# A planned order for attention and gated MLP on one core: loads tied to the first score, the last output unit in three parts

## The chip, the cores and the metric

The kernel runs on one core of a Trainium2 chip. The metric is the device time of one execution in microseconds (us). A core has five engines: PE (TensorE, with its weight loads shown apart as PEld), DVE (VectorE), ACT (ScalarE), POOL (GpSimd) and SP (SyncE), each with a queue of its own that runs in program order, and 16 DMA engines which all queues share. Matmul results land in PSUM and are copied to SBUF by DVE or ACT.

## The reference

Four batches, eight heads, 768 tokens, head dimension 64. An 8x8 matrix per head is normalized by rows and columns five times and then mixes the eight blocks of 96 tokens of k and v. Attention runs inside each block. Its output, 768x512 per batch, goes through a gated MLP whose gate mixes tokens.

```python
for _ in range(5):                       # P: (B, H, 8, 8)
    P = exp(P - max(P, -1)); P /= sum(P, -1) + 1e-9; P /= sum(P, -2) + 1e-9
k_s = einsum('bhij,bhjcd->bhicd', P, k_blocks)     # v_s in the same way
attn = softmax(q_b @ k_s.T / sqrt(64)) @ v_s       # within each block
x = attn as (4, 768, 512)
h = relu(x @ w_in)                       # 512 -> 1024
u, v = h[..., :512], h[..., 512:]
v_n = (v - mean(v)) / sqrt(var(v) + 1e-6)
v_s = einsum('ts,bsd->btd', w_spatial, v_n) + b_spatial
out = (u * v_s) @ w_out                  # 512 -> 512, float32
```

## The kernel before

The instruction order of PE, DVE, ACT and POOL is written out by hand in the string `SCHEDULE`. It is a list of units. A token such as `a20-3` reads: unit `a`, number 2, batch 0, engine that evicts the result (A for ACT, D for DVE, - for a fixed one), PSUM tile 3. There are four PSUM tiles (`ps0` to `ps3`, each two banks of 512 float32 columns), so a unit waits until the unit that last had its tile is evicted. The units and their matmuls (each with its weight load):

| token | method | matmuls | what follows |
|---|---|---|---|
| k, t | `mixed_t` (L302) | 12 | mixes and transposes k or v, evicted to `kT` |
| q | `qtr` (L290) | 24 | transposes q, evicted to `qT` |
| s | `score` (L345) | 8, 96 wide | exponential on ACT to `ex` (L352) |
| z | `sums` (L364) | 4, 384 wide | logarithm and exponential on ACT to `lns` (L370, L371) |
| a | `attend` (L382) | 32, 96 wide | two products on DVE to `xt` (L392) |
| B | `vblk` (L329) | 8 | evicted to `vb` |
| v | `vmix` (L260) | 2 | evicted to `vm`, written to DRAM and read back as `vb` by SP |
| X, V | `vstart`, `vproj` (L415) | 4 for X; 8 for V, or 4 behind its X | 512 wide; `relu` on ACT, statistics on DVE |
| N | `norm` | none | two steps on ACT, six on DVE (L448) |
| U | `uproj` (L458) | 8, 384 wide | `relu` on ACT or DVE |
| S | `spatial` (L474) | 12, 384 wide | bias on DVE (L485), product on POOL (L486) to `gt` |
| O | `oproj` (L496) | 8, 512 wide | evicted to `o_sb`, stored by SP |
| w | `wsp_unit` (L226) | 6 | transposes `w_spatial` |

Batches overlap: the attention of batch b+1 is interleaved with the MLP of batch b. A stage below means such a pair. `O` uses the `gt` of all four `S` units of its batch in the order in which they are numbered.

Loads of q, k and v are issued by POOL (`load_heads`, L94), with two buffers per tensor. Those of batches 0 and 1 and of the weights are issued at the start. Those of batch b+2 are issued behind the first `S` of batch b, so behind its product on POOL's queue:

```python
if name == "S" and b + 2 < B and len(gmlp[b].gt) == 1:
    v_in[b + 2] = load_heads(v, b + 2, "v_in")
    ...
```

In the last batch each `O` unit is evicted in four copies of 128x256, alternating DVE and ACT, and stored in two DMAs of 256 KB on SP's queue. All four copies of a unit read one PSUM tile and write one SBUF tile. `lns` has four buffers.

## Time and profile before

| | |
|---|---|
| runs, us | 159.97, 163.50, 163.62 (median 163.5) |
| profiled execution, us | 165.63; its span, first to last instruction, 163.8 |
| busy in the span, us | PE 147.0, PEld 85.6, DVE 93.3, ACT 95.8, POOL 47.9 |
| granted TensorE clock, mean | 0.962 |
| instructions | 4347, of them 1888 matmuls and 1897 weight loads in the trace |
| DMA | 23.88 MB moved; read 27.14 MB, written 8.65 MB of HBM |
| q, k, v of a batch | 768 KB each in SBUF; median 13.9, 10.6, 9.6 us from issue to landing |

Views of the profile used below: the slices (the span in 40 equal parts, a digit is a busy share in tenths, PEclk the clock that was granted to TensorE), the chain of waits (the work that ended last, followed back to what released each step; "issue" is time in which an engine waited for nothing that the profile shows), the windows (per stretch: busy time of PE, PEld, DVE, ACT, POOL, with the number of instructions in brackets, then the granted clock, the mean share of the DMA engines, and GB/s), and the groups of instructions by line with the mean time of one. In a DMA row the numbers are packets, MB and the share of 16 engines' time; q0 holds POOL's loads, q1 SP's transfers, q8 instructions. Matmuls are pipelined, so the price of one in a row of equal ones is read from the chain (16 of 512 columns in 3.45 us) and not from its own mean (406 ns).

### The profile page before, as it was taken

How to read it: one execution, taken by the hardware profiler on the slowest of the kernel's cores; microseconds unless marked ns; L12 is line 12 of the kernel's file. 1: busy time of each engine (PE TensorE's matmuls, PEld its weight loads, DVE VectorE, ACT ScalarE, POOL GpSimd, SP SyncE). 2: the span in 40 equal slices, each digit the busy share in tenths (PEclk: the TensorE clock that was granted, in tenths of full speed). 3: DMA queues.
4: the chain of work that ended last, by engine and by line, in shares of the span. 5: the costliest groups of instructions: out<-in, count | busy, mean ns of one | idle time of the engine just before them, and what ended most of it. 6: DMA issues, size and time to landing. Idle time of an engine off the chain costs nothing.

```text
span 163.8 us, 4347 instructions
## 1 busy us (share of the span) xinstructions
PE 147.0 (90%) x1888; PEld 85.6 (52%) x1897; DVE 93.3 (57%) x196; ACT 95.8 (59%) x147; POOL 47.9 (29%) x45
## 2 busy tenths in 40 slices
PE   0949887999999958999999999999999999999970
PEld 0237764366765543445855554458655454566430
DVE  4777895068954382039654385396543853844751
ACT  3167992088966670567986725679867346570040
POOL 7966920000006950000009750000045600005600
PEclk9999995599999996999999999999999999999997
DMA  2999999999590999651742999817500036000055
GB/s 13 197 204 211 221 260 192 202 204 208 162 238 20 134 204 203 194 233 59 211 118 14 174 203 223 352 39 223 132 0 0 4 134 256 0 0 0 6 192 193
DMA packets 21299, 23.88 MB, mean 146 GB/s; under 512 B 736, under 2 KB 18144, under 8 KB 21152
## 3 DMA queue, kind: packets, MB, share of 16 engines
q0 software_dynamic: 13504, 12.58, 47.9%
q1 hardware_dynamic: 7776, 11.02, 20.0%
q8 instruction: 15, 0.25, 0.6%
q14 instruction: 4, 0.03, 0.1%
HBM read 27.14 MB, written 8.65 MB: 219 GB/s over the span
## 4 chain that ended last, share of the span: by engine, by line
PE 77%; DVE 8%; ACT 5%; issue 4%; POOL 3%; DMA 1%; DVEq 0%; POOLq 0%
PE ps L474 19%; PE ps L415 14%; PE ps L458 13%; PE ps L496 12%; PE ps L345 4%; PE ps L302 3%; POOL gt L486 3%; ACT ex L352 3%; PE ps L290 3%; PE ps L260 2%; PE ps L382 2%; PE ps L364 2%; DVE vs L485 2%; PE ps L226 1%; PE ps L329 1%
## 5 line engine op out<-in xcount | busy, mean ns | idle before, releaser
L486 POOL TENSOR_TENSOR gt<-vs,u_sb 128x768 bf16<-128x768 f32 x15 | 24.6, 1647 | 99.4 <-ACT ex L352 73.9
L474 PE MATMUL ps<-wspT,v_sb 128*128 128x384 bf16 x192 | 33.5, 327 | 0.0
L485 DVE TENSOR_TENSOR vs<-ps,b_bc 128x768 f32<-128x768 f32 (+1 forms) x17 | 15.5, 910 | 24.5 <-PE ps L474 24.5
L437 DVE BATCH_NORM_STATS2 stats<-v_sb 128x6 f32<-128x512 bf16 x24 | 16.2, 675 | 22.9 <-ACT v_sb L241 22.8
L352 ACT ACTIVATE ex<-ps 96x768 bf16<-96x768 f32 x32 | 24.1, 804 | 7.7 <-PE ps L345 7.7
L474 PEld LDWEIGHTS <-v_sb 128*128 128x128 bf16 x192 | 17.8, 98 | 12.3 <-issue 1.0
L496 PE MATMUL ps<-w_out_sb,gt 128*128 128x512 bf16 x90 | 23.6, 403 | 0.6
L415 PE MATMUL ps<-w_in_sb,xt 128*128 128x512 bf16 x94 | 23.8, 406 | 0.2 <-issue 0.2
L458 PE MATMUL ps<-xt,w_in_sb 128*128 128x384 bf16 x128 | 23.0, 326 | 0.1
L235 ACT COPY o_sb<-ps 128x1024 f32<-128x1024 f32 (+1 forms) x13 | 9.3, 717 | 22.0 <-DVE o_sb L237 11.8
L241 ACT ACTIVATE v_sb<-ps 128x1024 bf16<-128x1024 f32 (+1 forms) x15 | 12.4, 852 | 11.7 <-PE ps L415 11.0
L392 DVE TENSOR_TENSOR xt<-ps,lns 128x384 bf16<-128x384 f32 x32 | 15.8, 549 | 3.6 <-PE ps L382 3.3
L458 PEld LDWEIGHTS <-w_in_sb 128*128 128x128 bf16 x128 | 12.1, 98 | 8.4
L415 PEld LDWEIGHTS <-xt 128*128 128x128 bf16 x96 | 9.9, 104 | 12.5 <-issue 3.0
L496 PEld LDWEIGHTS <-gt 128*128 128x128 bf16 x96 | 9.1, 102 | 12.8 <-issue 2.3
L370 ACT ACTIVATE lns<-ps 128x384 f32<-128x384 f32 x16 | 7.8, 488 | 11.0 <-PE ps L364 11.0
L382 PE MATMUL ps<-ex,vb 96*32 96x96 bf16 x512 | 8.7, 215 | 4.0 <-issue 3.7
L241 ACT ACTIVATE u_sb<-ps 128x768 bf16<-128x768 f32 x14 | 11.2, 813 | 1.8 <-PE ps L458 1.8
L235 ACT CAST kT<-ps 128x768 bf16<-128x768 f32 x14 | 10.6, 811 | 0.9 <-PE ps L302 0.9
L382 PEld LDWEIGHTS <-vb 96*32 96x32 bf16 x512 | 7.4, 101 | 5.1 <-issue 4.0
L345 PE MATMUL ps<-qT,kT 64*96 64x96 bf16 x256 | 9.6, 210 | 0.1
L345 PEld LDWEIGHTS <-kT 64*96 64x96 bf16 x256 | 7.2, 121 | 4.3 <-issue 3.5
(73 smaller groups left out, 157.8 us busy)
## 6 DMA issues: line engine op xcount, KB each, us to landing
out_dram<-o_sb SPq DMA_DIRECT2D x9, 512.0 KB, 2.7
q_in<-in_q_dram POOLq DMA_DIRECT2D x4, 768.0 KB, 13.9
k_in<-in_k_dram POOLq DMA_DIRECT2D x4, 768.0 KB, 10.6
v_in<-in_v_dram POOLq DMA_DIRECT2D x4, 768.0 KB, 9.6
vd<-vm SPq DMA_DIRECT2D x6, 384.0 KB, 2.5
vb<-vd SPq DMA_DIRECT2D x6, 384.0 KB, 4.3
out_dram<-o_sb SPq DMA_DIRECT2D x6, 256.0 KB, 2.1
wsp_nat<-in_moe_w_spatial_dram POOLq DMA_DIRECT2D x1, 1152.0 KB, 21.4
```

Of the source, the lines that this page charges most:

```text
L235: nc.scalar.copy(out=out, in_=in_)
L241: nc.scalar.activation(out=out, in_=in_, func=AF.Relu)
L345: nc.tensor.matmul(t[0:BLK, hh, ii * BLK:(ii + 1) * BLK], lhsT=self.k[hp][rows, i * BLK:(i + 1) * BLK], rhs=self.q[hp][rows, i], start=Tru ...
L352: nc.scalar.activation(out=e.rearrange("p h i c -> p h (i c)"), in_=t[0:BLK, :, 0:NB // 2 * BLK], func=AF.Exp, scale=scale,)
L382: nc.tensor.matmul(t[c * DQ:(c + 1) * DQ, dh, ii * BLK:(ii + 1) * BLK], lhsT=self.vb[:, i, j, c, :].rearrange("c (d x) -> c x d", x=2)[:, ...
L415: nc.tensor.matmul(self.vt[n][:, x, :], lhsT=self.xt(kc)[:, g * 128:(g + 1) * 128], rhs=w_in_sb[:, kc, DH:DFF], start=(kc == 0), stop=(kc ...
L437: nc.vector.bn_stats(out=stats, in_=v_sb[:, x, :])
L458: nc.tensor.matmul(t[:, x, 0:HW], lhsT=w_in_sb[:, kc, mc * 128:(mc + 1) * 128], rhs=self.xt(kc)[:, x * HW:(x + 1) * HW], start=(kc == 0), ...
L474: nc.tensor.matmul(t[:, x, 0:HW], lhsT=self.v[g][:, mc * 128:(mc + 1) * 128], rhs=wspT[:, g, x * HW:(x + 1) * HW], start=(g == 0), stop=(g ...
L485: nc.vector.tensor_add(out=vs[:, x], in0=t[:, x, 0:HW], in1=b2[:, x])
L486: eng.tensor_mul(out=gt2[:, x], in0=vs[:, x], in1=u2[:, x])
L496: nc.tensor.matmul(t[:, x, :], lhsT=self.gt[mc][:, g * 128:(g + 1) * 128], rhs=w_out_sb[:, mc, :], start=(mc == 0), stop=(mc == FC - 1),)
```

## The change

Three things change in the code, and the order of the units changes throughout.

- The loads of batch b+1 are issued behind the first `score` of batch b, for b of 1 and 2, and POOL first copies one element of that score's `ex` tile, which makes POOL's queue wait for ACT's exponential.
- The last `O` unit of the last batch is computed in three parts (512, 256 and 256 columns wide), each in a PSUM tile and an SBUF tile of its own, with one copy and one DMA for each: the first two by ACT and SP's queue, the third by DVE and ACT's queue. The other `O` units of the last batch are evicted in one copy and stored in one DMA of 512 KB.
- `lns` has three buffers in place of four.
- `SCHEDULE` has a new order. Among other things `X10` stands ahead of `a20` in batch 0, and `O10` and `O00` stand ahead of `a31` and `a21` of batch 1. Engines and PSUM tiles of the units are newly assigned; four more `relu`s are on DVE.

```diff
-    ln_pool = ctx.enter_context(tc.tile_pool(name="ln", bufs=4))
+    ln_pool = ctx.enter_context(tc.tile_pool(name="ln", bufs=3))
...
         def oproj(self, n, eng, ps):
+            self.ops.append(ps)
             t = ps_tile(ps)
...
             if self.last and n == G // 2 - 1:
-                pairs = [(mc, x) for x in range(2) for mc in range(FC)]
...
+                free = min(set(range(4)) - set(self.ops))
+                parts = ((0, 0, DM, t), (1, 0, DM // 2, ps_tile(free)), (1, DM // 2, DM // 2, None))
+                for x, c, width, tp in parts:
+                    tp = ps_tile(self.ops[0]) if tp is None else tp
+                    g = 2 * n + x
+                    for mc in range(FC):
+                        nc.tensor.matmul(
+                            tp[:, 0, 0:width], lhsT=self.gt[mc][:, g * 128:(g + 1) * 128],
+                            rhs=w_out_sb[:, mc, c:c + width],
+                            start=(mc == 0), stop=(mc == FC - 1),
+                        )
+                    o_x = o_pool.tile([128, width], FP32, name="o_x", tag=f"o{x}{c}", bufs=1)
+                    copy(DVE if c else ACT, o_x, tp[:, 0, 0:width])
+                    (nc.scalar if c else nc.sync).dma_start(
+                        out=o_dram[:, x, c:c + width], in_=o_x,
+                    )
+                return
...
-            if self.last:
-                for x in range(2):
-                    copy(DVE, o_sb[:, x, 0:DM // 2], t[:, x, 0:DM // 2])
-                    copy(ACT, o_sb[:, x, DM // 2:], t[:, x, DM // 2:])
-                    nc.sync.dma_start(out=o_dram[:, x, :], in_=o_sb[:, x, :])
-            else:
-                copy(eng, o_sb, t)
-                nc.sync.dma_start(out=o_dram, in_=o_sb)
+            copy(eng, o_sb, t)
+            nc.sync.dma_start(out=o_dram, in_=o_sb)
...
     SCHEDULE = """
-        k00A2 k10A3 k20D0 s00-1 s10-2 k30D3 s20-0 s30-1 t30D2 t00A3 t10D0 z10-1 t20D2 s50-3
-        B00D1 B10D0 s60-2 z00-3 B30D1 B20D0 s40-2 a00-3 s70-1 a10-0 z20-2 a20-3 z30-1 a30-2
-        X10-0 X00-1 V20-3 V00-- U10A2 w40A3 w30D1 V10-- w10A2 U30A3 v11D0 v31A1 U00A2 w50D3
-        v21A1 w20D0 k31D2 N00-- k01A3 v01A1 U20A0 k21A2 k11A3 q11D1 w00D0 q01D2 s51-3 s71-1
-        S00-0 s01-2 s21-3 S30-1 z01-0 z31-2 S10-3 s41-0 s11-1 S20-2 s61-3 a31-0 s31-1 a01-2
-        z21-3 z11-1 a21-0 a11-3 O20A2 O00A1 O10A0 V01-3 V11-2 v22A1 v32D0 V21-3 U11A2 v12A1
-        v02A3 U21A0 k22A2 q12D1 k02A3 q02D0 N01-- k32A2 k12A1 U31A3 s72-0 s02-2 S11-1 s52-3
...
+        k00A2 k10A3 k20D0 s10-1 s20-2 k30D3 s00-0 s30-1 t30D2 t10A3 t00D0 z10-1 t20D2 s40-3
+        B10D1 B00D0 z00-2 B30D3 s60-1 a10-2 a00-0 B20D3 s50-1 s70-2 z20-1 X10-0 z30-3 a20-2
+        a30-1 X00-3 V20-2 V10-- w30A1 V00-- U30A2 v11A0 v21A1 U20A3 w40D2 w10D0 N00-- U00A1
+        v01A3 U10A2 w20D0 w50D1 w00A3 k11D2 k31A0 q01D1 k01A3 q11A2 k21A0 v31A1 S00-3 s01-2
+        s11-0 S20-1 s51-3 s31-2 S10-0 z11-1 s21-3 S30-2 s61-1 a11-0 z01-3 a01-2 s71-1 s41-3
+        O10D0 z31-1 z21-2 O00A3 a31-1 a21-0 O20D2 V01-3 v12D1 v02A0 V11-2 v32A3 V21-0 v22A2
+        U01A1 k02A3 q12D0 k22A2 q02D1 k32A3 k12D0 U11D2 N01-- s42-1 s12-3 U21D0 s62-2 s02-1
+        S01-3 s32-2 s72-1 S11-0 s52-3 s22-2 S21-1 z02-0 z22-3 U31D2 z32-0 a32-1 S31-3 a22-2
...
     """
...
-                if name == "S" and b + 2 < B and len(gmlp[b].gt) == 1:
-                    v_in[b + 2] = load_heads(v, b + 2, "v_in")
-                    k_in[b + 2] = load_heads(k, b + 2, "k_in")
-                    q_in[b + 2] = load_heads(q, b + 2, "q_in")
             else:
                 getattr(attn[b], UNITS[name])(n, eng, ps)
+                if name == "s" and 1 <= b < B - 1 and len(attn[b].e) == 1:
+                    gate = small.tile([1, 1], BF16, name="gate", tag="gate")
+                    nc.gpsimd.tensor_copy(out=gate, in_=attn[b].e[n][0:1, 0, 0, 0:1])
+                    v_in[b + 1] = load_heads(v, b + 1, "v_in")
+                    k_in[b + 1] = load_heads(k, b + 1, "k_in")
+                    q_in[b + 1] = load_heads(q, b + 1, "q_in")
```

## The prediction

> **What bounds the kernel now.** I read the slices of the page first. TensorE (PE) is busy for 147.0 of 163.8 us, so a gain must come out of its gaps or out of its speed.

> ```profile
> PE   0949887999999958999999999999999999999970
> PEclk9999995599999996999999999999999999999997
> DMA  2999999999590999651742999817500036000055
> ```

> Each digit is a slice of 4.1 us. In slices 7 and 8 (24.6 to 32.8 us) and 16 (61.4 to 65.5) PE has a reduced clock; in both places its busy share dips just before, and the DMA row stands at 9. Next, the chain of waits around the two places: start, length, what ran.

> ```profile
> 23.82 0.26 PE ps L382 x6
> 24.09 1.47 issue
> 25.55 0.74 PE ps L382 x14
> 26.30 0.32 PE ps L364 x2
> 26.62 0.64 PE ps L382 x16
> 27.26 0.54 PE ps L415
> 27.80 0.22 issue
> 28.02 6.00 PE ps L415 x18
> ...
> 59.12 0.64 PE ps L382 x60
> 59.76 2.22 issue
> 61.99 0.23 PE ps L382 x4
> 62.22 0.32 PE ps L496
> 62.54 0.05 issue
> 62.59 6.60 PE ps L496 x22
> 69.19 0.86 PE ps L415 x4
> ```

> "issue" is time in which PE waited for no semaphore. Both times it stops in the middle of the small matmuls of `attend` (L382), and the wide matmuls behind it then run slowly. At full clock a 512-wide one takes 0.216 us (the chain has 3.45 us for 16 of L415 later on). 18 of them in 6.00 us and 22 in 6.60 us are 0.333 and 0.300.

> Why does PE stop? Windows that end at the stops count its instructions (PE matmuls and PEld weight loads):

> ```profile
> 0.00:24.09 24.09, 17.04 (x350) 11.55 (x351) 17.84 (x52) 15.27 (x24) 17.12 (x24) 1.00 1.05 184
> 0.00:59.76 59.76, 50.81 (x859) 32.76 (x862) 38.44 (x92) 37.95 (x59) 27.21 (x31) 0.94 1.00 177
> ```

> 701 and 1721 instructions: 1020 apart, four times 255 (some matmul records are missing). And the DMA view of 59 to 60.6 us shows a packet of the instruction queue among the loads; from 52 to 59.5 us there is none.

> ```profile
> q0 software_dynamic: 414, 0.32, 128.3%
> q8 instruction: 1, 0.02, 3.5%
> ```

> The queue brings 0.25 MB in 15 packets, so 16 KB each, 256 instructions of 64 bytes. I conclude that PE runs out of fetched code: the block arrives late behind batch loads. [...]

> **The losses by rows.** First place: 24.09 to 34.02 is 9.93 us; its work at full clock is 58 `attend` matmuls at 0.011 (0.34 us for 32 at 98.3 us), 4 `sums` matmuls in 0.3 and 20 wide ones at 0.216, together 5.3. **Loss 4.6**: 1.5 of stop, 3.1 of clock. Second: 59.76 to 69.19 is 9.43 us for 4 small and 24 wide, 5.2. **Loss 4.2**: 2.2 of stop, about 1.9 of clock. A windows view gives the clock as 0.50 for 25.14 to 31.97 and for 62.69 to 66.10, right behind the stops.

> [...] In this trace 1.47 and 2.22 us were enough, both times directly ahead of the half clock, while the 0.6 to 0.7 us waits at 96.7 and 129.7 left it at 1.00. I take the row: a stop above 1 us costs clock, one at 0.7 does not.

> **The change, part by part.**

> *Order.* A block is consumed between two stops 256 instructions (128 matmuls) apart, so I count the 128 matmuls ahead of the same instruction number in both orders. Second place, before: 112 of `attend` and `score` (1.3 us), 8 of `sums` (0.7) and some rest, nominally 2.3 us; the trace has 57.15 to 59.76, 2.6, and PE went on 4.8 us after 57.15. After the change these 128 hold 84 of `attend`, 16 of `score`, 12 of `sums`, and O10 and O00, 16 wide matmuls of 3.45 us: nominally 5.9, with the same 0.3 of waits 6.2. That exceeds the 4.8 by 1.4, so the stop goes. First place: in the new order X10 (4 wide, 0.86 us) stands ahead of a20 and one `sums` more, 1.0 us in all; before, the block lasted from 19.45 to 24.09 (4.6), and PE went on 6.1 after 19.45. After: 5.6, which leaves a stop of 0.5. By the 0.7 us waits that costs no clock. Other blocks have 7 us and more, or no loads beside them.

> *What is late next at the first place.* The loads for batch 1 do not move. The q load is issued on POOL at 9.93 and takes 30.7 us (the longest of its row), landing at 40.6. The first batch-1 `qtr` ran at 44.75; without 4.6 and 0.8 earlier by the order it would start at 39.35. It waits 1.25 us. (`vmix`'s load lands at 8.17+24.7=32.9 and v11 would come at 32.0: a wait inside the same 1.25.) The 0.5 us stop is covered by it. **First place: 4.6-1.25 = 3.3.**

> *Gate and loads on POOL.* For batch 2 nothing moves: S00's product (L486, 1.65 us), then a 1x1 copy, then three DMA issues (0.95, 0.88, 0.90), then the products of S20, S10, S30. No row shows such a copy on POOL; a 128x1 memset there takes 0.11, a 128x768 copy 1.56; I take 0.2, being nearer the first. The gate waits for the exponent of s01. ACT has five evictions queued ahead, done about 1 us before S00's product ends, so at nothing; without that cover every us would delay the products of S20, S10 and S30 behind it. O10 now stands right behind the `attend` work, 8 units sooner. S00's matmuls would end at 45.4; product until 48.3, gate 48.5, issues until 51.2, three products until 56.2. O10 starts at 54.7 and needs S30's product after 6 of its 8 matmuls, at 56.0. **Wait 0.2**, between 0 and 1. For batch 3 the loads move ahead of S01, some 5 us sooner, while POOL is idle: nothing on the path. **Second place: 4.2-0.2 = 4.0.**

> *`lns` with three buffers.* In every batch a fourth `sums` follows at least one `attend`: nothing. The four `relu`s more on DVE (0.96 us each, DVE busy 57%) stand beside PE work: nothing; should they not fit, a norm (six of 0.33 us) starts 0.9 late, with 2.3 us ahead of its use.

> *Tail.* Before: the last matmul ends at 158.82 and four copies run one after the other, DVE 0.44, ACT 0.38, DVE 0.43, ACT 0.37; the last DMA issues at 160.58, 1.76 us behind the matmul. After: ACT copies O13 whole (1.01), then 512 columns (0.37 for 256 and 1.01 for 1024 give 0.59), then 256 (0.37), ending about 0.35 behind the last matmul; DVE's 256 (0.42) run beside. The issue rows are 0.33 each; two on SP queue for at most 0.4, that on ACT stands behind its copies. Last issue at +0.45 to +0.8. **Gain 1.0**, between 0 (the 512 KB of O13 leave late and 1 MB lands together) and 1.3. The halved matmuls stream the same columns, 4 matmuls more, 0.01 each.

> **Sum.** The profiled execution took 165.63 (span 163.8). 165.63-3.3-4.0-1.0 = 157.3. The runs were 159.97, 163.5 and 163.62. Taking both clock losses out of the profiled one gives 165.63-5.0 = 160.6, the first one left in 163.7: I read the runs as executions with none and one, and set them 0.3 below the profiled. **Forecast 157.0 us.** About 2% of 163.5 is what a measurement of this kernel can tell from no change.

> **The rivals.**

> *The clock still drops at the first place* (20%). A stop of 0.5 beside small matmuls may do what 1.5 did. For: 1.05 us of idle before 25.14 was enough. Against: X10 fills the stretch. Then 0.5+3.1 instead of the covering 1.25: 157.0+2.35 = 159.4.

> *The change does not do what it says* (6%). If the stops come wherever `attend` runs under full DMA, not by count, both stay; only the tail gains: 162.5. Against: four `attend`s at 98 us under a DMA at 9 ran through.

> *The blocks come still later* (6%), the slower side: output stores of O10 and O00 now join the loads around 55 to 60 us. Were blocks 2 us later (8.1 and 8.2 after the request), the stops would be 2.5 and 2.0; each with two stretches of half clock (3.1 and 3.6) that gives 157.0-1.25+2.5+3.1+2.0+3.6 = 167.0. It passes 163.5 once both stops exceed 1 us, at some 7 us per block; 6.1 is the most measured.

> **How the numbers follow.** The forecast's case has 68%. Its own range is 155.2 (tail 1.3, none of the 1.25) to 158.6 (O10 waits 1, no tail gain). The range reaches to the first rival: 155.2 to 160.4. Over 2% faster is below 160.2: nearly all of the forecast's case; the first rival lies close to the bound, and I count a quarter of it. Faster 72%, within 2% 22%, slower 6%.

> **What would show it.** Right: no "issue" over 1 us on PE, granted clock 1.00 from 8 us to the tail, O10 and O00 at 0.216 per matmul, `qtr` of batch 1 waiting for its load near 40.6, the last DMA issue within 0.8 of the last matmul. Wrong: "issue" of 1 us or more near instruction 701 or 1721, or PE waiting over 1 us for POOL at O10.

## The result, and the profile after

The changed kernel takes 158.89 us (median of 12, 158.13 to 160.27), the kernel before 163.51 (median of 15, 159.97 to 165.76). The ratio is 0.9855, 95% interval 0.9797 to 0.9913. It sets the twelve against the four quickest executions of the kernel before (159.97 to 161.97), so it is nearer to 1 than the medians, which give 0.972. A second measurement of the same kernel, told below, gave 158.62 and 0.9743 (0.9681 to 0.9804). The forecast was 157.0 with a range of 155.2 to 160.4: the time lies in it, but the gain is 4.6 us between medians where 6.5 were forecast, and against those four executions only 2.3.

The profiled execution took 159.66 us, its span is 157.8; before it was 165.63 and 163.8. The slices of the changed kernel:

```profile
PE   0958998999999999999999999999999999999970
PEclk9998579999999999999999999999999999999999
DMA  2999999999845999976499927258000054000054
```

The two half-clock places of before are gone. There is a new one in slices 4 to 6 (a window gives 0.50 for 14.54 to 21.37 us), behind a wait of PE for the normalization, 1.91 us long, that ends at 12.26 us, and a run of small matmuls. PE's work up to 12.26 us is the same in both kernels. Seven of the twelve executions have a mean clock of 0.99 or more, this one 0.978. The second place, in the chain of waits of the changed kernel:

```profile
55.05 0.53 PE ps L382 x32
55.58 0.49 PE ps L345 x16
56.07 0.32 PE ps L515
56.39 0.05 issue
56.44 1.46 PE ps L515 x6
57.90 0.44 PE ps L364 x8
58.34 1.83 PE ps L515 x8
60.17 0.58 PE ps L382 x44
60.75 0.14 issue
60.90 0.40 PE ps L382 x20
61.30 0.32 PE ps L515
```

O10 and O00 (L515, 16 wide matmuls, one of them missing in the trace) stand ahead of a31 and a21 (L382). The stop of 2.22 us has become 0.14. It is still there, and at the same count: the windows view up to it has 857+861 = 1718 instructions of PE and PEld; before it was 1721.

```profile
0.00:60.75 60.75, 53.38 (x857) 34.31 (x861) 38.05 (x91) 41.92 (x63) 27.36 (x32) 0.94 1.03 182
```

Where the 6.0 us between the two profiled executions came from, by the start of units: S00's first matmul 47.1 before, 44.1 after (3.0); from there to the first `vproj` of batch 1 21.9 and 18.9 (3.0); from there to the last matmul 89.4 and 89.5; from there to the end of the span 5.32 and 5.31 (0.0).

### The profile page after: what moved, and what is told of

It reads as the page before. It is cut to its first block, busy times and chain, and to the rows that moved or that the text cites. A ratio compares the mean times of both kernels' runs of the same rounds, so it can differ in the third digit from the quotient of the medians.

```text
span 157.8 us, 4336 instructions
## 1 busy us (share of the span) xinstructions
PE 144.6 (92%) x1892; PEld 85.8 (54%) x1901; DVE 97.9 (62%) x197; ACT 92.7 (59%) x139; POOL 48.5 (31%) x47
## 4 chain that ended last, share of the span: by engine, by line
PE 83%; DVE 8%; ACT 2%; issue 1%; POOLq 1%; DMA 1%; DVEq 0%
PE ps L474 19%; PE ps L458 14%; PE ps L415 13%; PE ps L515 12%; PE ps L302 5%; PE ps L345 5%; PE ps L382 3%; PE ps L290 3%; PE ps L260 3%; DVE vs L485 2%; PE ps L364 2%; PE ps L329 1%; PE ps L226 1%; PE ps L501 1%; DMA p_all<-in_sort_net_dram 1%
## 5 line engine op out<-in xcount | busy, mean ns | idle before, releaser
L486 POOL TENSOR_TENSOR gt<-vs,u_sb 128x768 bf16<-128x768 f32 x15 | 24.6, 1646 | 72.6 <-DVE vs L485 50.4
L415 PE MATMUL ps<-w_in_sb,xt 128*128 128x512 bf16 x93 | 22.3, 379 | 0.2
L515 PE MATMUL ps<-w_out_sb,gt 128*128 128x512 bf16 x83 | 19.9, 380 | 0.4
L235 ACT COPY o_sb<-ps 128x1024 f32<-128x1024 f32 x7 | 7.1, 1012 | 18.0 <-PE ps L515 18.0
L415 PEld LDWEIGHTS <-xt 128*128 128x128 bf16 x96 | 9.1, 98 | 10.6 <-DVE xt L392 0.4
L515 PEld LDWEIGHTS <-gt 128*128 128x128 bf16 x88 | 7.9, 98 | 10.2 <-POOL gt L486 1.2
L345 PE MATMUL ps<-qT,kT 64*96 64x96 bf16 x256 | 10.5, 222 | 0.2
L235 ACT CAST kT<-ps 128x768 bf16<-128x768 f32 x12 | 9.4, 800 | 1.7 <-PE ps L302 1.7
L237 DVE CAST kT<-ps 128x768 bf16<-128x768 f32 x8 | 7.6, 955 | 2.9 <-PE ps L302 2.8
L448 DVE TENSOR_SCALAR v_sb<-v_sb,mv,rstd 128x512 bf16<-128x512 bf16 x24 | 8.3, 416 | 0.6 <-ACT rstd L446 0.6
L371 ACT ACTIVATE lns<-lns 128x384 f32<-128x384 f32 x16 | 8.4, 523 | 0.5
```

What stands on the lines that cost most here:

```text
L235: nc.scalar.copy(out=out, in_=in_)
L345: nc.tensor.matmul(t[0:BLK, hh, ii * BLK:(ii + 1) * BLK], lhsT=self.k[hp][rows, i * BLK:(i + 1) * BLK], rhs=self.q[hp][rows, i], start=Tru ...
L415: nc.tensor.matmul(self.vt[n][:, x, :], lhsT=self.xt(kc)[:, g * 128:(g + 1) * 128], rhs=w_in_sb[:, kc, DH:DFF], start=(kc == 0), stop=(kc ...
L486: eng.tensor_mul(out=gt2[:, x], in0=vs[:, x], in1=u2[:, x])
L515: nc.tensor.matmul(t[:, x, :], lhsT=self.gt[mc][:, g * 128:(g + 1) * 128], rhs=w_out_sb[:, mc, :], start=(mc == 0), stop=(mc == FC - 1),)
```

## The experiments

The theory is the prediction's reading of its trace: PE runs out of fetched instructions at fixed counts. The rivals: PE stops wherever `attend` runs under full DMA; the new place of the loads made the gain; the tail made it. `SB` and `SA` below stand for the orders before and after.

**The new order alone.**

```diff
-    SCHEDULE = SB
+    SCHEDULE = SA
```

> The kernel before with the new SCHEDULE alone; loads, last unit and lns buffers as before. If the gain comes from PE no longer running out of fetched instructions, nearly all of it is here: no stop of 1 us or more on PE, 158.5 to 160.0 us, 0.97 to 0.98 of the kernel before. If it comes from the loads or the tail, this stays within 1% of the kernel before (162 to 165).

Four executions: 159.20, 159.25, 164.02, 164.99 beside 163.62 of before. No stop of 1 us in the profiled one, which was one of the long ones (164.99). It waits for something else:

```profile
PE ps L382 <- DMA vb<-vd: 3.7, 1, 3.7
```

That is a wait which the prediction does not name: `attend` of batch 1 for the second reload of v. A stretch of half clock of 6.8 us lies behind it. So the order alone brings nearly all of the gain, in two of four executions, and something new in the other two. With the new issue point of the loads as well, executions of 162.8 us and more are not gone: 5 of 30 (the twelve above and the six each of the changed kernel again, with the old tail, and with the halves). Four executions are too few to say how much the issue point does.

**The new issue point of the loads alone.**

```diff
-                if name == "S" and b + 2 < B and len(gmlp[b].gt) == 1:
-                    v_in[b + 2] = load_heads(v, b + 2, "v_in")
...
+                if name == "s" and 1 <= b < B - 1 and len(attn[b].e) == 1:
+                    gate = small.tile([1, 1], BF16, name="gate", tag="gate")
+                    nc.gpsimd.tensor_copy(out=gate, in_=attn[b].e[n][0:1, 0, 0, 0:1])
```

> The kernel before with the new issue point of the loads alone. In the old order the first score of batch 1 stands ahead of S00, so the loads of batch 2 start some 4 us sooner and still cover the instruction block that runs out near 59.8 us. Fetch theory: both stops stay (1.5 and 2.2 us, the second up to 1 us shorter), 162.5 to 164. If the place of the loads made the gain: 159 to 160.

163.17, ratio 0.9990 (0.9945 to 1.0035). Both stops stay, 1.22 and 1.86 us. In the old order it is worth nothing.

**The new tail alone**, with `lns` in three buffers.

```diff
-            if self.last:
-                for x in range(2):
-                    copy(DVE, o_sb[:, x, 0:DM // 2], t[:, x, 0:DM // 2])
...
+                parts = ((0, 0, DM, t), (1, 0, DM // 2, ps_tile(free)), (1, DM // 2, DM // 2, None))
```

> The kernel before with the last output unit of the changed kernel (three parts, the two units ahead of it stored whole, lns with three buffers). The prediction's theory, that the end is set by the four copies in a row: 1.0 us less. The rival, that the end is set by 1 MB of stores which now start later together: 0.2 us less to 0.3 more, 163 to 164, with the last landing at most 0.5 us nearer to the last matmul than before.

162.81 in the median of 6 beside 163.62; ratio 0.9897 (0.9820 to 0.9975). The spread of the executions is wider than the question, so the trace decides: the last landing comes 3.71 us behind the start of the last matmul, before 4.17. The gain at the landing is 0.46 us, nearly what the rival named as its most. This trace also shows something that bears on the whole forecast: with the old order, PE stops for 1.57 us at the first place and keeps its full clock. The part on why the prediction failed comes back to it.

**The old order with 128 instructions more in front.**

```diff
+    def tiny(n, ps):
+        t = ps_tile(ps)
+        for _ in range(n):
+            nc.tensor.matmul(t[0:32, 0, 0:32], lhsT=ident_bf[:, 0:32], rhs=warm_sb[:, 0:32], start=True, stop=True)
...
         attn[0].qtr(0, ACT, 2), attn[0].qtr(1, ACT, 3)
+        tiny(64, 1)
         warm(2, 1)
```

> The kernel before, in its own order, with 64 tiny matmuls more (32 columns, 128 PE instructions, result not used) at a place where PE waits for the first normalization. Every unit thereby stands 128 instructions later, so that a block of 256 ends at another unit. Fetch theory: near instruction 701 PE is then within a00 and a10, and near 1721 behind S10 and S20, whose 24 wide matmuls are in the block that counts; the second stop goes, the first shrinks below 1 us or moves 64 matmuls ahead: 158.5 to 161. Rival, that PE stops wherever attend runs under full DMA: both stops stay in a20 and a11, 163.5 to 165.

162.61, ratio 0.9939 (0.9910 to 0.9968), not the 158.5 to 161 that I expected. The second stop went, as expected; the first did not shrink. There is no stop in `attend` any more, neither in batch 0 nor in batch 1; the only one stands in a wide matmul (L420 here is `vproj`). Chain of waits of this kernel:

```profile
24.27 0.53 PE ps L387 x32
24.79 0.16 PE ps L369 x4
24.96 0.34 PE ps L387 x32
25.30 0.32 PE ps L420
25.62 3.16 issue
28.78 7.14 PE ps L420 x19
```

Its windows view counts 957 instructions up to there, one block of 256 behind the 701 of before:

```profile
0.00:25.62 25.62, 19.71 (x478) 14.01 (x479) 18.78 (x54) 16.36 (x27) 18.04 (x24) 1.00 1.06 187
```

A stop in the middle of a 512-wide unit, at a block's count, is no property of `attend`; that rival is out. I had not asked what becomes late one block further on: by the count, the whole `attend` work of batch 0 fell into one block, and the stop behind it, in X10, took 3.2 us in place of 1.5.

**No loads of batches 2 and 3.**

```diff
-                    v_in[b + 2] = load_heads(v, b + 2, "v_in")
-                    k_in[b + 2] = load_heads(k, b + 2, "k_in")
-                    q_in[b + 2] = load_heads(q, b + 2, "q_in")
+                    v_in[b + 2], k_in[b + 2], q_in[b + 2] = v_in[b], k_in[b], q_in[b]
```

> The kernel before without the loads of batches 2 and 3: their attention takes the q, k and v of batches 0 and 1 again, so the output of these batches is that of other data; the instructions of PE, DVE and ACT and their order are the same. If the batch loads delay the instruction block: the stop near 59.8 us shrinks from 2.2 to below 0.3 us and the clock stays, the first stop, beside the loads of the start, remains: 158.5 to 161. If the stop belongs to the order alone: both remain, 162 to 164.

159.66 (158.35 to 161.24, four executions), ratio 0.9763 (0.9677 to 0.9848). The order on PE is that of before, and the second place now runs through at full clock; the first stop, beside the loads of the start, stays (1.21). Chain of waits:

```profile
57.15 0.35 PE ps L364 x4
57.50 0.68 PE ps L382 x64
58.18 0.35 PE ps L496
58.53 0.05 issue
58.59 4.91 PE ps L496 x22
```

So the loads delay the block. From 56 to 58 us the DMA engines stand still here (share 0.00), and PE runs at a clock of 1.00. Before, with the loads, PE enters the block ahead of the stop at 57.15, the next packet starts among the loads at 59.55, and PE goes on at 61.99.

**The changed kernel with the old tail.**

```diff
-                    copy(DVE if c else ACT, o_x, tp[:, 0, 0:width])
...
+                    copy(DVE, o_sb[:, x, 0:DM // 2], t[:, x, 0:DM // 2])
+                    copy(ACT, o_sb[:, x, DM // 2:], t[:, x, DM // 2:])
+                    nc.sync.dma_start(out=o_dram[:, x, :], in_=o_sb[:, x, :])
```

> The changed kernel with the last batch's output units of the kernel before (four copies of 128x256 and two stores for each unit). The prediction's sum: 1.0 us slower than the changed kernel. The theory after the first traces, that the stores and not the copies set the end: the last landing comes 4.2 us behind the start of the last matmul (3.7 in the changed kernel), so 0.4 to 0.5 us slower.

158.92 to 159.68 in five executions, 164.72 in one; median 159.39. The last landing is 4.17 behind the start of the last matmul, as expected. Its profiled execution has full clock from 8.4 us to the tail and shows the wait that the prediction set behind the first stop:

```profile
9.93 30.77 DMA q_in<-in_q_dram
40.70 0.04 issue
40.74 0.86 PE ps L290 x24
```

**The last unit but one in halves.**

```diff
+            if self.last and n == 1:
+                for x in range(2):
+                    o_h = o_pool.tile([128, 2, DM], FP32, name="o_sb", tag="o")
+                    copy(ACT if x else DVE, o_h[:, 0, :], t[:, x, :])
+                    nc.sync.dma_start(out=o_dram[:, x, :], in_=o_h[:, 0, :])
+                return
```

> The changed kernel with the last unit but one evicted in two halves of 128x512 by DVE and ACT beside each other, each in an SBUF tile of its own and with a store of 256 KB of its own; the last unit stays in three parts. If the 512 KB store of that unit, issued 0.4 us ahead of the last matmul, holds up the three behind it, they now land sooner: last landing 2.9 to 3.4 us behind the start of the last matmul in place of 3.7, 0.3 to 0.8 us faster. If the fixed time of a store sets the end, 3.6 to 3.8 as now.

157.76, 158.18, 159.40 and 162.87, 163.96, 164.64; the profiled one is that of 162.87 and waits 3.5 us for vb. The last landing comes at 3.47 behind the start of the last matmul in place of 3.71: between what the two theories expected. 0.24 us belonged to the queue of stores; whether the rest is the fixed time of a store is not shown. Of the tails tried, the best is worth 0.7 us at the landing, the one in the change 0.46.

**The new order with later loads.**

```diff
-                if name == "S" and b + 2 < B and len(gmlp[b].gt) == 1:
+                if name == "S" and b + 2 < B and len(gmlp[b].gt) == 2:
```

> The kernel before with the new SCHEDULE, the loads of a batch issued behind the second spatial unit of a stage in place of the first. The new order alone had PE wait 3.7 us for vb, because the loads were issued at 48.2, ahead of the store-and-reload of v at 49.0. If that collision is what the new issue point avoids, later loads avoid it too: attend of batch 1 waits for vb less than 0.5 us, no stretch of half clock behind it, 158.5 to 160 in every execution. If the wait belongs to the order: a 3 to 4 us wait for vb remains.

159.73 to 160.66, median 160.15, at the upper end of what I expected and a little above it. In the profiled one vb is issued at 49.3, the loads at 51.0; no wait for vb and no half clock. It costs elsewhere: the q load of batch 2 lands at 71.2, and the transposes wait 0.9 us for it.

**The changed kernel again, and beside it v31 ahead of k11.** The second kernel has the halves too.

```diff
-        w00A3 k11D2 k31A0 q01D1 k01A3 q11A2 k21A0 v31A1 S00-3 s01-2
+        w00A3 v31A1 k11D2 k31A0 q01D1 k01A3 q11A2 k21A0 S00-3 s01-2
```

> The changed kernel once more, beside the one above on the same chip. Its profiled execution had half clock from 14.5 to 21.4 us, so its units, and the loads with them, came later, and vb was issued 0.4 us ahead of the loads. Without that stretch vb and the loads are issued within 0.5 us of each other and some executions wait for vb: 158.1 to 160.3 in most, 163 to 165 in one of five or fewer; PE's first batch-1 transposes of q then wait for their load near 40.7, as the prediction has it.

> The changed kernel with the last unit but one stored in halves, and with v31 (the unit that starts the second store-and-reload of v for batch 1) moved from just ahead of S00 to ahead of k11. The reload of vb would be issued near 46.6 in place of 49.0, ahead of the loads of batch 2 at 48.2. If the wait for vb in part of the executions is this collision, it is gone in all of them: no wait for vb over 0.5 us, every execution between 157.5 and 159.7, median 158.4. If the wait has another cause, half of the executions stay at 163 to 165.

The changed kernel: 158.12, 158.36, 158.55, 158.69 and 161.27, 164.91. The 164.91 was the profiled one, so the collision can be read; the 161.27 stays unexplained. On SP's queue (timeline), the second reload waits for its store, 3.4 us:

```profile
46.03 0.33 SPq L277 DMA_DIRECT2D vd<-vm  x1
49.45 0.32 SPq L278 DMA_DIRECT2D vb<-vd  x1
```

On POOL's queue the gate (0.18 us) and the loads come 0.7 us before it:

```profile
48.60 0.18 POOL L576 COPY gate<-ex 1x1 bf16<-1x1 bf16 x1
48.73 0.96 POOL L94 DMA_DIRECT2D v_in<-in_v_dram  x1
49.67 0.88 POOL L94 DMA_DIRECT2D k_in<-in_k_dram  x1
```

And the chain of waits shows what that costs. The reload takes 8.3 us; in the first profiled execution, issued 0.4 us ahead of the loads, it took 4.2. With the old tail it was issued 0.5 us behind the first of the loads and took 4.9, and PE waited 0.4 us for it. So the margin between the harmless case and this one is small. The 8 wide matmuls of O10 behind it run at half clock (0.50 from 56.26 to 63.09).

```profile
46.03 3.40 DMA vd<-vm
49.43 0.02 issue
49.45 8.32 DMA vb<-vd
57.77 0.14 issue
...
60.49 3.13 PE ps L515 x8
```

With v31 early all six executions lie between 158.01 and 159.30, median 158.35. But vb was issued at 49.12, not at 46.6: its store stood behind the first reload on SP. The loads were issued at 49.03. The reload landed at 53.5, and PE did not wait. The margin I had meant to make was not there, and six executions without a long one say little: the changed kernel's first twelve had none either.

**The stores of v by ACT, in all batches.**

```diff
-                nc.sync.dma_start(out=vd, in_=self.vm[:, half].rearrange("p g h d -> p (g h d)"))
+                nc.scalar.dma_start(out=vd, in_=self.vm[:, half].rearrange("p g h d -> p (g h d)"))
```

> The changed kernel with the last unit but one in halves, v31 ahead of k11 as before, and the stores of the mixed v (vd) issued by ACT behind its copies, so that SP's queue holds only the reloads (vb) and the second store need not stand behind the first reload. The run with v31 moved alone issued the second vb at 49.1, not at 46.6 as I had expected, because its store stood behind the first reload on SP. Now both reloads should be issued by 46 and land by 51, 2 us ahead of the loads of batch 2 and 3 us ahead of attend: no wait for vb over 0.3 us, all executions 157.4 to 159.5.

160.91 to 162.23, median 161.06: a miss. Both reloads were issued by 45.2 and landed by 49.6, no wait for vb, granted clock 1.00. But in batch 2 the store waits for a copy of DVE, and ACT's queue with it. ACT's timeline:

```profile
65.15 0.79 ACT L235 CAST vm<-ps 128x768 bf16<-128x768 f32 x1
67.92 0.33 ACTq L277 DMA_DIRECT2D vd<-vm  x1
68.30 1.02 ACT L241 ACTIVATE v_sb<-ps 128x1024 bf16<-128x1024 f32 x1 [2.35 <-DVE vm L237]
```

**The loads ahead of the reload.** In the changed kernel POOL waits for an earlier tile:

```diff
-                if name == "s" and 1 <= b < B - 1 and len(attn[b].e) == 1:
+                if name == "k" and n == 2 and 1 <= b < B - 1:
...
-                    nc.gpsimd.tensor_copy(out=gate, in_=attn[b].e[n][0:1, 0, 0, 0:1])
+                    nc.gpsimd.tensor_copy(out=gate, in_=attn[b].k[n][0:1, 0:1])
```

> The changed kernel with POOL's one-element copy reading the kT of k21 of the stage's later batch in place of the first score's ex, so that the loads of batch 2 are issued near 44, some 5 us ahead of the second reload of vb. If loads ahead of the reload are what makes PE wait: every execution now waits 2 to 4 us for vb, with half clock behind it in most: 161.5 to 165, no execution at 158. If the long executions of the changed kernel have another cause: 158 to 160 in most, as in the changed kernel.

165.97 to 168.61, median 166.81, ratio 1.0184 (1.0122 to 1.0246): every execution is slower than the median of the kernel before beside it (163.74), and by more than I expected. In the profiled one the loads are issued at 45.4, the second vb at 49.5; it lands at 59.6. The waits of PE:

```profile
PE ps L382 <- DMA vb<-vd: 6.3, 1, 6.3
```

**The reload early for batch 1 alone**: with the rest as in the kernel before but the order, and then with the changed kernel and the halves.

```diff
-                nc.sync.dma_start(out=vd, in_=self.vm[:, half].rearrange("p g h d -> p (g h d)"))
+                (nc.scalar if self.b == 1 else nc.sync).dma_start(out=vd, in_=self.vm[:, half].rearrange("p g h d -> p (g h d)"))
...
-        w00A3 k11D2 k31A0 q01D1 k01A3 q11A2 k21A0 v31A1 S00-3 s01-2
+        w00A3 v31A1 k11D2 k31A0 q01D1 k01A3 q11A2 k21A0 S00-3 s01-2
```

> The new SCHEDULE with the loads, the last units and lns as in the kernel before; v31 stands ahead of k11, and for batch 1 alone ACT issues the stores of the mixed v, right behind its own copies. If the wait for vb is all that the new place of the loads avoids: no wait for vb over 0.3 us, no execution at 163 to 165, 158.3 to 159.5. If the loads matter in another way: still 163 to 165 in part of the executions.

> The changed kernel with the last unit but one in halves, v31 ahead of k11, and ACT's issue of the vd stores in batch 1 alone. In all batches it cost ACT 2.4 us behind a copy of DVE in batch 2 and as much in batch 3 (161.0), which falls away. Both reloads land before 50, the loads of batch 2 are issued near 48.8: no wait for vb, no stop over 0.7 us, granted clock 1.00 in most: 157.3 to 158.3, the fastest kernel of this study, about 0.97 of the kernel before. If the forecast of 157.0 missed by another cause than vb and the stores: 158.3 as the changed kernel without disturbance.

The first: 159.25 to 160.33, median 159.60, just above what I expected; no wait for vb, the old place of the loads (48.6) and the old tail. Against the new order alone only the reload has moved, with v31 and its store (it lands at 49.9 in place of 57.0), and none of the four executions is at 164. The second: 157.92 to 159.34, median 158.22, ratio 0.9717 (0.9668 to 0.9765): the lowest median of this study, and inside what I expected, at the upper end. It is 0.7 us below the changed kernel's first twelve, which had no long execution either, so the wait for vb does not explain that difference.

## Why the prediction was right or wrong

**The step that failed: what the first place costs, and with it the base.** The mechanism held; the size of the gain did not. I priced the first place at 4.6 us, 3.1 of it clock, from one profiled execution, and I read the runs of the kernel before as executions with none and with one of the two clock losses. But the half clock at the first place is no fixed price. It lasted 6.8 us in that execution (165.63). Two of the runs above keep the old order and were profiled too: the new issue point alone (163.52) had 3.4 us of it, and the new tail alone (161.39) had none; both have the second half clock. Their PEclk rows:

```profile
PEclk9999997899999996999999999999999999999997
PEclk9999999999999978999999999999999999999999
```

S00 begins accordingly: its first matmul is at 47.1 us in the kernel before, at 45.4 and 43.8 in these two, and at 44.1 in the changed kernel. The pieces of the four chains, in this order:

```profile
47.17 2.06 PE ps L474 x12
45.50 2.06 PE ps L474 x12
43.88 2.06 PE ps L474 x12
44.26 1.95 PE ps L474 x12
```

In every trace the q load of batch 1 lands at 40.2 to 41.2 us, and S00 never begins sooner than 2.5 us behind it. So ahead of S00 the change saved 3.0 us against the longest case, 1.3 against the middle one, and nothing against an execution without half clock there (0.9 more in each case where the changed kernel has full clock from the start and begins S00 at 43.2). Only the second place gains in every pair: from S00 to the first `vproj` the three take 21.4 to 21.9 us, the changed kernel 18.9. That roughly fits a gain of 4.6 us between medians and of 2.3 against the four quickest executions. Those four were not profiled, so that they had no half clock at the first place is inferred, and why the same stop is followed by 6.8, 3.4 or 0 us of it stays open. Against their mean (161.4) even 157.0 would have been 2.7% and not 4%.

**What bounds PE: right.** The stops move with the count (701 instructions in the kernel before, 957 with 128 more in front) and go with the loads (2.22 us at the second place, none without the loads of batches 2 and 3). 957 lies 256 behind 701, and 1721 four times 255. The row of the instruction queue agrees: 15 packets of 16 KB for the 3785 instructions of PE and PEld in the trace, 252 for each. And the packets come late: up to the second stop of the kernel before, each starts 1.1 to 4.1 us after PE has entered the block ahead of it, the one for the stop at 1721 at 59.55 where PE entered at 57.15. That PE had then run out of fetched instructions is my conclusion from counts and packets; no row names it.

**Stops and clock: right for most of these stops, wrong as a rule.** In the profiled executions eight stops of 1.2 to 3.2 us were seen: seven had half clock behind them, of 3.4 or 6.8 us, one of 1.57 (the new tail alone) had none. Four waits for vb of 3.5 to 6.3 us all had it. Stops of 0.14 and 0.69 had none. But "a stop above 1 us costs clock" does not hold for PE's other waits. Fourteen times, by the waits of the profiled executions, PE waited 1.0 to 1.9 us for the normalization or for a load of v, and only two of these waits (1.50 and 1.91 us, both ending near 12.3 us) had half clock behind them. One of the twelve others stands in the very trace that I read, ahead of 12.26 us, with the clock at 1.00 until 25.14:

```profile
PE ps L206 <- DVE mask L149: 1.7, 1, 1.7
```

What else has to come together with a stop is not shown, and neither is a length that is safe: 1.21 us beside small matmuls (no loads of batches 2 and 3) were followed by half clock, 1.57 (the new tail alone) were not.

**Order, second place: right in kind, without the margin.** I took 4.8 us from PE's entry into a block to the arrival of the next one, as at this place in my trace, and a block of 6.2, so 1.4 to spare. The block's 128 matmuls ran in 6.3 and PE still stopped for 0.14, because it went on 6.5 us after its entry. The profiled gain of this stretch is 3.0 (3.5 with the 0.5 by which S00 stands earlier in the new order, which the sum had put into the first place); forecast 4.0. The rest is at O10: it starts 11.9 us behind S00, not 11.3, and the chain ahead of it goes through S30's bias addition on DVE.

**What is late next at the first place: right, for the execution that it was worked out on.** `qtr` starts at 40.74, at the landing of its load, where the execution has full clock from the start, and S00 then at 43.2, 3.9 sooner than before; with 0.5 for the order the net is 3.4, forecast 3.3. In the profiled execution of the changed kernel the early half clock leaves 3.0, so a net of 2.5.

**Gate and loads on POOL: the price was right (0.18 for 0.2), the step was wrong.** "For batch 2 nothing moves" looked at POOL's queue alone. The new order moves v31 to just ahead of S00, and with it a store and a reload on SP's queue, next to the loads. Of a moved unit I had counted the matmuls and the copy, and not its two DMAs. That term was 0. In the traces it is 0 where the reload is issued first or within 0.1 us of the loads, 0.4 us where it comes 0.5 us behind them, and 3.5 to 4.1 us plus half clock where it comes 0.7 or 0.8 us behind. Further kernels show it from both sides: loads 4 us ahead (6.3 us of wait, 166.8), the reload early in batch 1 (no wait in either of the two), and later loads (no wait). In the twelve executions of the result no time was as long as with this wait, so this step was wrong, but it is not what the twelve fell short by.

**Tail: wrong in size.** I priced the copies and took the store's time from the row. The copies did shrink, from 2.11 to 0.73 us behind the start of the last matmul. The end of the chain in the changed kernel, where one copy is left:

```profile
151.02 1.75 PE ps L501 x12
152.77 0.02 issue
152.79 0.42 DVE o_x L237
```

But the store of 512 KB of O13 leaves at 152.1 and three stores stand behind it: the last on SP's queue is issued 0.52 behind the last matmul's start and takes 3.2 us to land, before it was 2.14 and 2.0. 0.46 us are left of the 1.0. In the profiled pair even these do not show, since the program's end came 1.16 us behind the last landing before and 1.60 after. That is not scatter, for it goes with the kernel: 1.14 to 1.22 in all five traces of the old order, with either tail, 1.55 to 1.69 in eight traces of the new one, and 1.14 to 1.16 in the three that have v31 early and the halves. What takes these 0.44 us stays open.

**The sum.** Forecast 8.3 of the profiled 165.63, measured 6.0. Missing: 0.8 at the first place (the early half clock), 0.5 at the second, 1.0 at the tail. The 0.8 is no constant either: of the twelve executions the five with a mean clock under 0.99 have a median of 159.58, the other seven 158.70, and their ranges overlap. The rivals: clock still dropping at the first place, blocks coming still later, and no effect did not happen. A fourth that I had not listed did, in part of the later executions: a transfer that takes the place of the wait removed.

## What to carry to other kernels

When a hand-made order moves a unit, follow its DMAs as well as its engine work, and look at what will be issued in the same microsecond on another queue; a reload 0.7 us or more behind 2.3 MB of loads took 7.8 to 10.0 us in four traces, in place of 4.2. Do not price a clock loss from one profile: the same order showed 6.8, 3.4 and 0 us of half clock at one place, and the slowest execution promised the largest gain. Here PE stopped for 1.2 to 3.2 us in or behind long runs of very small matmuls under heavy loads, at 701, 957 and 1721 instructions where they were counted: count instructions up to a stop that waits for nothing, and mix wide matmuls into the block that ends there. Price a tail by the landing of the last byte, with what is queued ahead of it, and not by the last copy.

## What the runs showed of the hardware that I had not expected

A one-element copy on POOL took 0.18 and 0.21 us in the changed kernel, 0.18 in its second measurement.

Between start and tail, the stretches of half clock whose ends were read lasted 3.41, 6.83 or 10.24 us: 6.83 and 3.41 in the kernel before, 6.83 in the changed kernel and in its second measurement, 10.24 with the loads ahead of the reload. At the first place a stop of 1.47 us stood ahead of 6.83 us of half clock, which cost 3.1 us more; a stop of 1.57 us with the new tail alone stood ahead of none.
